# Where the low parts of a pair of hidden blocks are taken, and where w_in's sums stand, in a pooled-attention and squared-ReLU kernel

## The chip, the cores and the metric

The kernel runs on one core of one Trainium2 chip. The metric is the time of one execution in microseconds (us), the median of three runs. A profile is one more execution, recorded by the hardware profiler: its *span* goes from the first to the last instruction of the program, and its own time, as the runs are timed, includes a little around that span.

The engines of a core run side by side, each with its own queue of instructions in program order: TensorE (PE in the profile; PEld is its loading of weights), VectorE (DVE), ScalarE (ACT), GpSimd (POOL) and SyncE (SP), which issues most of the DMAs. They wait for each other through semaphores.

## The reference

Attention over keys and values that are pooled by eight, then a feed-forward block with a squared ReLU. `q`, `k`, `v` are 8 x 8 x 576 x 64 (batch, heads, sequence, width), `w_in` is 512 x 2048, `w_out` 2048 x 512, all in float32.

```python
def _attn_ref(q, k, v) -> np.ndarray:
    ...
    k_p = k.reshape(B, H, Sp, pool, D).mean(axis=3)
    v_p = v.reshape(B, H, Sp, pool, D).mean(axis=3)
    scores = scale * np.matmul(q, k_p.transpose(0, 1, 3, 2))
    scores = scores - np.max(scores, axis=-1, keepdims=True)
    attn = np.exp(scores)
    attn = attn / (np.sum(attn, axis=-1, keepdims=True) + 1e-09)
    return np.matmul(attn, v_p).astype(np.float32)

def _moe_ref(x, w_in, w_out) -> np.ndarray:
    h = np.maximum(x @ w_in, 0.0)
    return (h * h @ w_out).astype(np.float32)
```

The 4608 rows of attention output, 512 wide, are the `x` of the second function.

## The kernel before

**Chunks, blocks, steps.** The 4608 tokens are cut into nine chunks `c` of 512, the 2048 hidden columns into sixteen blocks `fc` of 128. A *step* is one chunk and one block, in the order of `steps` (line 625): step `s = 16 c + fc`. In step `s` TensorE makes block `s` of the hidden layer (`hidden`, lines 566 to 584) and then multiplies block `s - 3` with its part of `w_out` (`project`, lines 603 to 622; the 3 is `LAG`).

**Low and high parts.** From chunk 1 on each float32 operand is split in two numbers that TensorE multiplies fast: a high part (a cast on ScalarE) and a low part (the operand less its high part, on VectorE). Three products of four are made. The square of a hidden block, `r`, is so split into `gh` and `gl` by `split_hidden` (lines 586 to 594): ScalarE casts `r` into `gh` at once; the subtraction that makes `gl` is put on the list `behind`. `catch_up` (lines 176 to 178) empties that list. `r` has two buffers, `gh` and `gl` three each.

**Seven products for a pair.** Chunks 0 and 1 (`PLAIN` is 2) take each block alone (`plain`). From chunk 2 on, thus from step 32 on, `seven` (lines 526 to 564) makes two blocks at once with seven products in place of eight: an even step makes four products into two PSUM tiles X and Y and lets VectorE combine their halves (`soon`: a copy u on ScalarE, then u, h, h on VectorE; `at_end`: a second copy u, then h), the odd step makes three more. Only then are both blocks complete, and `activate` takes ReLU and square of both, r and r, on ScalarE. TensorE's next even step needs the PSUM tiles that these two free: X after the first, Y after the second.

**Operands for the seven.** `w_in` is needed in eight forms: four are its quarters (`split_quarter`, named w_A in the profile), four are sums of quarters, made in place on VectorE by `sum_of_quarters` (lines 189 to 194; wf_i) and then split by `split_operand` (lines 180 to 184; w_S). The sixteen sums are scheduled one a step, from step 27 on (line 727). The input `x` is likewise summed (xf) and split (x_B, x_T) in the last steps of the chunk before.

**Attention** for the next chunks is done between these: for each pair of heads of a chunk, `transpose_q` (qs, st) in one step, `scores` two steps later (sps, then copies sc on ScalarE, then the maximum mx over the 72 partitions on GpSimd), `exponents` two steps further (sc minus mx on VectorE, the exponential on ScalarE, then the sum tot over partitions on GpSimd), then `send_sums`, `fetch_sums`, `reciprocals`, `fetch_reciprocals` through memory (rs, rc, rr, rd, rb), and `weigh_values` (av, xf). From step 32 on scores and exponentials fall in even steps.

**What sets the order.** Every engine's order is written out: the loop over `s` (lines 763 to 810) calls the parts of a step one after the other. The places that matter here, in order: `hidden` for TensorE; fetches of weights; `split_hidden` of step `s - 2` (line 772); `project` of `s - 3`; in odd steps `catch_up` (line 778); `soon`, which in an odd step is `activate`; the ScalarE and VectorE parts of attention that follow a product; `at_end`; `catch_up` (line 785); loads; the other scheduled work; `activate` where it is not in `soon` (chunks 0 and 1); sums and operands of x, reciprocals, sums of quarters. Buffers of weights (tag "w", 40 of them) are handed out in that order as they come free, and whoever writes one waits for its last reader.

Of the kernel before, what the change touches and what calls it, by code (L numbers as in the profile page):

```python
# [37 lines left out]
def pooled_attn_relu2_ffn(  # L38
# [25 lines left out]
    NFC = DFF // P  # L64
# [8 lines left out]
    PLAIN = 2  # L73
# [31 lines left out]
    def issue_loads():  # L105
        for dst, src in loads:
            dma(dst, src)
        loads.clear()
# [6 lines left out]
    def w_tile(dt, name):  # L115
        return wts.tile([P, 2, 512], dt, name=name, tag="w", bufs=SLOTS)
# [39 lines left out]
    def to_float32(*keys):  # L156
        parts = []
        for key in keys:
            words, m = raw.pop(key).rearrange("p a (n w) -> p a n w", w=2), wf[key]
            parts.append((words, m, m.bitcast(U32)))  # L160
        for _, m, _ in parts:
            DVE.tensor_scalar(m, m, EXP_MIN, EXP_MAX, op0=ALU.max, op1=ALU.min)
        for words, _, m in parts:
            DVE.scalar_tensor_tensor(m, m, 3, words[..., 0], op0=ALU.logical_shift_left, op1=ALU.bitwise_or)
        for words, _, m in parts:
            DVE.scalar_tensor_tensor(m, words[..., 1], 0x80000000, m, op0=ALU.bitwise_and, op1=ALU.bitwise_or)

    def in_blocks(t):
        return t.rearrange("p (c r n) -> p c r n", c=2, r=GB // 2)

    def quarter(g, e, kh):
        return both(g, kh).rearrange("p c (r e n) -> p e c r n", r=GB // 2, e=2)[:, e]

    behind = []

    def catch_up():
        while behind:
            behind.pop(0)()

    def split_operand(g, name, src):  # L180
        t = wt[g, name] = w_tile(F32R, f"w_{g}_{name}")
        hi, lo = in_blocks(t[:, 0, :]), in_blocks(t[:, 1, :])
        ACT.copy(hi, src)
        behind.append(lambda: DVE.tensor_tensor(lo, src, hi.bitcast(F32), op=ALU.subtract))
# [4 lines left out]
    def sum_of_quarters(g, name):  # L189
        (e, kh), a, b, op = {"S1": ((1, 1), (1, 0), (1, 1), ALU.add), "S3": ((1, 0), (0, 0), (1, 0), ALU.subtract),  # L190
                             "S2": ((1, 1), (1, 1), (0, 0), ALU.subtract), "S4": ((0, 1), (0, 1), (1, 1), ALU.subtract)}[name]
        t = quarter(g, e, kh)
        DVE.tensor_tensor(t, quarter(g, *a), quarter(g, *b), op=op)
        behind.append(lambda: split_operand(g, name, t))

    stored = {}

# [368 lines left out]
    def hidden(c, fc):  # L566
        if c < PLAIN:
            hps = [(fc, plain(c, fc))]
        else:
            hps = seven(c, fc)  # L570
            if fc % 2 == 0:
                return hps

        def activate():
            for f, hp in hps:
                if c == 0:
                    r = gts[c, f] = sb.tile([P, CH], F32, name=f"r_{c}_{f}", tag="gl" if f % 2 else "gh", bufs=3)
                else:
                    r = gts[c, f] = sb.tile([P, CH], F32, name=f"r_{c}_{f}", tag="r", bufs=2)
                ACT.activation(r, hp, AF.Relu)  # L580
            for f, _ in hps:
                ACT.activation(gts[c, f], gts[c, f], AF.Square)

        return (activate, None, None) if c >= PLAIN else (None, None, activate)

    def split_hidden(c, fc):
        if c == 0:
            return
        gh = sb.tile([P, CH], F32R, name=f"gh_{c}_{fc}", tag="gh", bufs=3)
        gl = sb.tile([P, CH], F32R, name=f"gl_{c}_{fc}", tag="gl", bufs=3)  # L590
        r = gts[c, fc]
        gts[c, fc] = (gh, gl)
        ACT.copy(gh, r)
        behind.append(lambda: DVE.tensor_tensor(gl, r, gh.bitcast(F32), op=ALU.subtract))

    accs, outs = {}, []

    def send_outs():
        for dst, src in outs:
            dma(dst, src)  # L600
        outs.clear()

    def project(c, fc):
        if fc == 0:
            accs[c] = [ps_o.tile([P, 512], F32, name=f"o_{c}_{t}", tag=f"o{t}") for t in range(NTT)]
        g, key = gts.pop((c, fc)), ("o", fc)
        for t in range(NTT):
            tt = slice(t * P, (t + 1) * P)
            if c == 0:
                prods = [(g[:, tt], wf[key].rearrange("p a n -> p (a n)"))]  # L610
            else:
                prods = [(g[x][:, tt], wt[key][:, w, :]) for x, w in three]
            for i, (a, w) in enumerate(prods):
                PE.matmul(accs[c][t], lhsT=a, rhs=w, start=fc == 0 and i == 0, stop=fc == NFC - 1 and i == len(prods) - 1)

        def store():
            for t in range(NTT):
                ob = half_tile("ob", f"ob_{c}_{t}")
                ACT.copy(ob, accs[c][t])
                outs.append((out[c * CH + t * P:c * CH + (t + 1) * P, :], ob))  # L620

        return store if fc == NFC - 1 else None


    steps = [(c, fc) for c in range(NCH) for fc in range(NFC)]
    work = {}

    def at(step, f, *a):
        work.setdefault(max(step, -PRO), []).append((f, a))
# [22 lines left out]
    t = ps_a.tile([P, 512], F32, name="stir", tag="a")  # L652
# [60 lines left out]
    t = 1e9  # L713
    for key in reversed(keys):
        t = min(t - 1 / RATE, need[key] - 1 - MARGIN)
# [7 lines left out]
    for i in range(NFC):  # L723
        at(12 + i, split_quarter, i // GB, i % GB // 2, i % 2)
        at(10 + i, store_weights, i)
        at(11 + i, send_weights, i)
        at(27 + i, sum_of_quarters, i // 4, ("S1", "S3", "S2", "S4")[i % 4])
        for c in range(1, NCH):
            at(c * NFC + i + LAG - STREAM, fetch_weights, c, i)

# [11 lines left out]
    for c in range(1, NCH):  # L742
# [10 lines left out]
        for p in range(NPAIR):  # L753
            s = c * NFC + first[p]
# [3 lines left out]


    last = (to_float32, split_quarter, sum_of_quarters, store_weights)  # L760
    on_pe = (turn_k, scores, token_scores, token_turn, weigh_values)
    store = None
    for s in range(-PRO, len(steps) + LAG):
        todo = work.get(s, [])
        soon, then, activate = hidden(*steps[s]) if 0 <= s < len(steps) else (None, None, None)
        later = [f(*a) for f, a in sorted(((f, a) for f, a in todo if f in on_pe), key=lambda x: x[0] is weigh_values)]
        for kind in (fetch_sums, fetch_weights):
            for f, a in todo:
                if f is kind:
                    f(*a)  # L770
        if 0 <= s - 2 < len(steps):
            split_hidden(*steps[s - 2])
        if store:
            store()
            send_outs()
        store = project(*steps[s - LAG]) if s >= LAG else None
        if s % 2:
            catch_up()
        if soon:
            soon()  # L780
        for f in later:
            f()
        if then:
            then()
        catch_up()
        first = (load_q, load_sums)
        for f, a in todo:
            if f is fetch_reciprocals:
                f(*a)
        for f, a in todo:  # L790
            if f in first:
                f(*a)
        issue_loads()
        for f, a in todo:
            if f not in first + on_pe + last + (x_sums, x_operand, reciprocals, fetch_weights, fetch_sums, fetch_reciprocals, first_sums):
                f(*a)
        keys = [a[0] for f, a in todo if f is to_float32]
        if keys:
            to_float32(*keys)
        for f, a in todo:  # L800
            if f in last[1:] and f is not sum_of_quarters:
                f(*a)
        issue_loads()
        if activate:
            activate()
        for kind in (x_sums, x_operand, reciprocals, sum_of_quarters, first_sums):
            for f, a in todo:
                if f is kind:
                    f(*a)
        issue_loads()  # L810
# [32 lines left out]
```

## Time and profile before

| | before |
|---|---|
| median of three runs | 943.03 us (942.89 to 944.5) |
| the profiled execution, timed as a run | 941.49 us |
| its span | 939.7 us |
| VectorE busy | 584.8 us, 62% of the span |
| ScalarE busy | 509.1 us, 54% |
| GpSimd busy | 425.5 us, 45% |
| mean granted clock of TensorE | 0.975 |

Busy times are sums of an engine's instructions. A bracket behind a row of the timeline tells how long the engine stood idle before that row and what ended the wait. All lines of the program go through one helper, line 34, so rows are told apart by the names of their tiles: `gl<-r,gh` writes gl from r and gh. A pair of steps, one even and one odd, takes 11 to 17 us; chunk 2 begins at about 267 us of the span, chunk 3 at about 370 us.

### The profile page before, as it was taken

How to read it: one execution, taken by the hardware profiler on the slowest of the kernel's cores; microseconds unless marked ns; L12 is line 12 of the kernel's file. 1: busy time of each engine (PE TensorE's matmuls, PEld its weight loads, DVE VectorE, ACT ScalarE, POOL GpSimd, SP SyncE). 2: the span in 40 equal slices, each digit the busy share in tenths (PEclk: the TensorE clock that was granted, in tenths of full speed). 3: DMA queues.
4: the chain of work that ended last, by engine and by line, in shares of the span. 5: the costliest groups of instructions: out<-in, count | busy, mean ns of one | idle time of the engine just before them, and what ended most of it. 6: DMA issues, size and time to landing. Idle time of an engine off the chain costs nothing.

```text
span 939.7 us, 14134 instructions
## 1 busy us (share of the span) xinstructions
PE 902.5 (96%) x5050; PEld 721.0 (77%) x5050; DVE 584.8 (62%) x971; ACT 509.1 (54%) x1015; POOL 425.5 (45%) x234
## 2 busy tenths in 40 slices
PE   4799999999999999999999999999999999999998
PEld 3344444577778878888888888888888878889997
DVE  4884887466777877665867576657645764453321
ACT  2477557565556555654565556555645564344343
POOL 6662225455553666565565555566444444200000
PEclk6589999999999999999999999999999999999999
DMA  8894654688655545756565566655433343344501
GB/s 193 253 271 91 145 163 152 153 228 222 165 123 137 141 102 148 183 142 137 125 172 145 134 145 174 145 132 125 158 113 114 113 157 102 102 163 170 218 1 45
DMA packets 161623, 138.72 MB, mean 148 GB/s; under 512 B 98776, under 2 KB 126424, under 8 KB 161552
## 3 DMA queue, kind: packets, MB, share of 16 engines
q1 hardware_dynamic: 132752, 127.13, 44.6%
q0 software_dynamic: 28800, 10.68, 10.0%
q8 instruction: 40, 0.66, 0.3%
q14 instruction: 31, 0.25, 0.1%
HBM read 119.65 MB, written 18.06 MB: 147 GB/s over the span
## 4 chain that ended last, share of the span: by engine, by line
PE 73%; DVE 12%; ACT 7%; issue 4%; DMA 2%; SPq 1%; POOL 0%; DVEq 0%; ACTq 0%
PE o L34 33%; PE h L34 32%; PE av L34 3%; DVE gl L34 3%; PE sps L34 3%; ACT sc L34 2%; SPq L34 1%; DVE st L34 1%; ACT r L34 1%; DMA raw_i<-in_moe_w_in_dram 1%; DVE h L34 1%; DVE wf_i L34 1%; DVE xf L34 1%; ACT x_T L34 1%; DVE x_T L34 1%
## 5 line engine op out<-in xcount | busy, mean ns | idle before, releaser
L34 PE MATMUL o<-w_o,gh 128*128 128x512 f32 x1024 | 322.1, 396 | 0.0
L34 POOL PARTITION_ALL_REDUCE tot<-sc x56 | 187.5, 3397 | 84.9 <-issue 84.2
L34 PEld LDWEIGHTS o<-w_o,gh 128*128 128x128 f32 x1024 | 184.4, 188 | 44.0 <-issue 7.2
L34 PE MATMUL o<-w_o,gl 128*128 128x512 f32 x512 | 199.5, 390 | 0.0
L34 POOL PARTITION_ALL_REDUCE mx<-sc x56 | 115.4, 2098 | 81.4 <-ACT sc L34 76.7
L34 ACT ACTIVATE r<-h 128x512 f32<-128x512 f32 x144 | 85.5, 597 | 118.0 <-PE h L34 55.8
L34 PE MATMUL h<-x_T,w_S 128*128 128x256 f32 x1008 | 133.9, 286 | 8.2 <-ACT r L34 7.3
L34 DVE TENSOR_TENSOR gl<-r,gh 128x512 fp32r<-128x512 f32 x128 | 123.4, 977 | 27.5 <-ACT gh L34 27.3
L34 PEld LDWEIGHTS h<-x_T,w_S 128*128 128x128 f32 x1008 | 127.0, 194 | 10.2 <-ACT r L34 8.5
L34 PEld LDWEIGHTS o<-w_o,gl 128*128 128x128 f32 x512 | 96.1, 188 | 21.2
L34 DVE TENSOR_TENSOR h<-h,u 128x256 f32<-128x256 f32 x168 | 72.6, 432 | 54.5 <-ACT u L34 29.5
L34 PE MATMUL h<-x_B,w_A 128*128 128x256 f32 x672 | 98.7, 283 | 5.6 <-ACT r L34 5.6
L34 PEld LDWEIGHTS h<-x_B,w_A 128*128 128x128 f32 x672 | 91.9, 191 | 10.6 <-ACT r L34 6.4
L34 ACT COPY u<-h 128x256 f32<-128x256 f32 x112 | 41.7, 373 | 103.3 <-DVE h L34 59.0
L34 POOL DMA_DIRECT2D k<-in_k_dram x36 | 44.6, 1239 | 106.7 <-issue 47.9
L34 POOL DMA_DIRECT2D v<-in_v_dram x36 | 44.0, 1223 | 96.8 <-issue 44.8
L34 ACT ACTIVATE r<-r 128x512 f32<-128x512 f32 x144 | 84.2, 625 | 1.0
L34 DVE TENSOR_TENSOR st<-qs,st 64x512 fp32r<-64x512 f32 x56 | 44.7, 797 | 63.7 <-ACT st L34 62.9
L34 DVE TENSOR_TENSOR u<-h,u 128x256 f32<-128x256 f32 x56 | 23.2, 415 | 92.7 <-ACT u L34 92.6
L34 ACT CAST gh<-r 128x512 fp32r<-128x512 f32 x128 | 78.6, 614 | 0.8 <-PE o L34 0.4
L34 ACT ACTIVATE sc<-sc 72x512 f32<-72x512 f32 x56 | 34.5, 631 | 52.2 <-DVE sc L34 52.2
L34 PE MATMUL h<-x,wf_i 128*128 128x512 f32 x128 | 60.0, 614 | 0.1
(89 smaller groups left out, 1207.7 us busy)
## 6 DMA issues: line engine op xcount, KB each, us to landing
w_o<-kept SPq DMA_DIRECT2D x128, 512.0 KB
out_dram<-ob SPq DMA_DIRECT2D x36, 256.0 KB
raw_i<-in_moe_w_in_dram SPq DMA_DIRECT2D x16, 512.0 KB
raw_o<-in_moe_w_out_dram SPq DMA_DIRECT2D x16, 512.0 KB
kept<-w_o SPq DMA_DIRECT2D x16, 512.0 KB
rb<-rd SPq DMA_DIRECT2D x56, 128.0 KB
k<-in_k_dram POOLq DMA_DIRECT2D x36, 144.0 KB, 4.8
v<-in_v_dram POOLq DMA_DIRECT2D x36, 144.0 KB, 4.3
```

Source lines behind the costliest of these rows:

```text
L34: return lambda *a, **k: self.tc.keep_in_program_order(f(*a, **k))
```

## The change

`split_hidden` is no longer called for every block two steps after it was made. A new function, `split_at`, is called at two places of the step: at the old one with block `s - 2`, and behind `soon` with block `s - 1`. It splits an odd block of chunk 2 or later at the second place, one step after its pair was made, and every other block at the old place. So both blocks of a pair are cast in the even step behind it, and both gl are taken by the `catch_up` at the end of that even step.

The sums of w_in's quarters are scheduled from step 26 on. Their split is put on a new list, `summed`, which the loop empties behind `activate`: the cast w_S stands at the end of the step after the sum, and its low part is taken by the first `catch_up` of the step after that.

```diff
-    behind = []
+    behind, summed = [], []
...
         DVE.tensor_tensor(t, quarter(g, *a), quarter(g, *b), op=op)
-        behind.append(lambda: split_operand(g, name, t))
+        summed.append(lambda: split_operand(g, name, t))
...
         behind.append(lambda: DVE.tensor_tensor(gl, r, gh.bitcast(F32), op=ALU.subtract))
+
+    def split_at(s, f):
+        if 0 <= f < len(steps) and s - f == (1 if f % 2 and f >= PLAIN * NFC else 2):
+            split_hidden(*steps[f])
...
-        at(27 + i, sum_of_quarters, i // 4, ("S1", "S3", "S2", "S4")[i % 4])
+        at(26 + i, sum_of_quarters, i // 4, ("S1", "S3", "S2", "S4")[i % 4])
...
-        if 0 <= s - 2 < len(steps):
-            split_hidden(*steps[s - 2])
+        split_at(s, s - 2)
         if store:
             store()
             send_outs()
...
         if soon:
             soon()
+        split_at(s, s - 1)
         for f in later:
             f()
...
         if activate:
             activate()
+        while summed:
+            summed.pop(0)()
```

What this makes of the queues, at three places. In the names the last number is a buffer's; of the numbers before it the last is the block, or the operand's own index.

The first place is ScalarE at the start of chunk 3, steps 48 and 49, where chunk 2's last pair (blocks 14 and 15) is cast; - is before, + is with the change.

```order
 L34 CAST gh_14_3376<-r_14_3323 128x512
 L34 COPY u_3_0_3372<-h_0_3346 128x256
+L34 CAST gh_15_3395<-r_15_3325 128x512
 L34 COPY u_3_0_3373<-h_1_3347 128x256
-L34 ACTIVATE sc_1_3259<-sc_1_3259 72x512 x2
-L34 CAST st_2_3421<-qs_2_3419 64x512 x2
-L34 CAST gh_15_3452<-r_15_3325 128x512
+L34 ACTIVATE sc_1_3262<-sc_1_3262 72x512 x2
+L34 CAST st_2_3425<-qs_2_3423 64x512 x2
 L34 ACTIVATE r_0_3468<-h_0_3346 128x512
 L34 ACTIVATE r_1_3470<-h_1_3347 128x512
```

The cast of block 15 has moved from just ahead of the new pair's r to between the two copies u of the even step. The same place on VectorE:

```order
 L34 TENSOR_TENSOR gl_14_3377<-r_14_3323,gh_14_3376 128x512
-L34 TENSOR_TENSOR sc_1_3259<-sc_1_3259,mx_1_0_3260 72x512
-L34 TENSOR_TENSOR sc_1_3259<-sc_1_3259,mx_1_1_3261 72x512
-L34 STREAM_TRANSPOSE qs_2_3419<-q_2_3129 128x512
-L34 TENSOR_TENSOR st_2_3421<-qs_2_3419,st_2_3421 64x512 x2
-L34 TENSOR_TENSOR gl_15_3453<-r_15_3325,gh_15_3452 128x512
-L34 TENSOR_TENSOR xf_0_3444<-av_0_3445,rb_0_3398 128x512
+L34 TENSOR_TENSOR gl_15_3396<-r_15_3325,gh_15_3395 128x512
+L34 TENSOR_TENSOR sc_1_3262<-sc_1_3262,mx_1_0_3263 72x512
+L34 TENSOR_TENSOR sc_1_3262<-sc_1_3262,mx_1_1_3264 72x512
+L34 STREAM_TRANSPOSE qs_2_3423<-q_2_3133 128x512
+L34 TENSOR_TENSOR st_2_3425<-qs_2_3423,st_2_3425 64x512 x2
```

Block 15's gl stood behind sc, qs and st; it now stands directly behind block 14's and ahead of them.

The second place is ScalarE in steps 32 and 33, the first pair of chunk 2. Before:

```order
L34 COPY u_2_0_2252<-h_1_2226 128x256
L34 CAST w_S_2276<-wf_i_1_506 128x512
L34 ACTIVATE sc_1_2137<-sc_1_2137 72x512 x2
L34 CAST st_2_2303<-qs_2_2301 64x512 x2
L34 CAST gh_15_2335<-r_15_2205 128x512
L34 CAST w_S_2350<-wf_i_0_479 128x512
L34 ACTIVATE r_0_2354<-h_0_2225 128x512
L34 ACTIVATE r_1_2356<-h_1_2226 128x512
```

With the change:

```order
L34 COPY u_2_0_2255<-h_1_2229 128x256
L34 ACTIVATE sc_1_2140<-sc_1_2140 72x512 x2
L34 CAST st_2_2304<-qs_2_2302 64x512 x2
L34 CAST w_S_2309<-wf_i_0_479 128x512
L34 CAST gh_15_2338<-r_15_2206 128x512
L34 ACTIVATE r_0_2355<-h_0_2228 128x512
L34 ACTIVATE r_1_2357<-h_1_2229 128x512
```

The cast w_S from wf_i_0_479 stands ahead of gh, and its sum was made one step earlier. VectorE there, before:

```order
L34 TENSOR_TENSOR st_2_2303<-qs_2_2301,st_2_2303 64x512 x2
L34 TENSOR_TENSOR wf_i_0_479<-wf_i_0_479 128x4x128
L34 TENSOR_TENSOR gl_15_2336<-r_15_2205,gh_15_2335 128x512
L34 TENSOR_TENSOR w_S_2350<-wf_i_0_479,w_S_2350 128x512
L34 TENSOR_TENSOR xf_0_2327<-av_0_2328,rb_0_2280 128x512
```

With the change:

```order
L34 TENSOR_TENSOR st_2_2304<-qs_2_2302,st_2_2304 64x512 x2
L34 TENSOR_TENSOR wf_i_1_506<-wf_i_1_506,wf_i_0_479 128x4x128
L34 TENSOR_TENSOR w_S_2309<-wf_i_0_479,w_S_2309 128x512
L34 TENSOR_TENSOR gl_15_2339<-r_15_2206,gh_15_2338 128x512
L34 TENSOR_TENSOR xf_0_2330<-av_0_2331,rb_0_2281 128x512
```

The sum in this place is now that of the next operand, and gl_15, a block of chunk 1, has changed places with the low part of w_S.

The third place is ScalarE in steps 42 and 43, where the last w_S is cast. Before:

```order
L34 COPY u_2_10_2963<-h_11_2937 128x256
L34 CAST w_S_3004<-wf_i_1_968 128x512
L34 CAST gh_9_3035<-r_9_2930 128x512
L34 CAST w_S_3050<-wf_i_1_968 128x512
L34 ACTIVATE r_10_3054<-h_10_2936 128x512
L34 ACTIVATE r_11_3056<-h_11_2937 128x512
```

With the change:

```order
L34 COPY u_2_10_2966<-h_11_2940 128x256
L34 CAST w_S_3017<-wf_i_1_968 128x512
L34 ACTIVATE r_10_3054<-h_10_2939 128x512
L34 ACTIVATE r_11_3056<-h_11_2940 128x512
```

The last cast w_S, block 9's gh and the w_S before it have all left the stretch between the even step's second copy and r; what stands there is the last w_S alone, in the even step. Its buffer is another one too: before, it came from the weights of block 8, which step 43's `project` reads, now from those of block 7, read in step 42.

## The prediction

> **What bounds the kernel now.** I read the page first, then TensorE's own waits, then the waits of all engines, then the timeline around each stall. TensorE is busy for 96% of the span and carries 73% of the chain, so the change can only win what TensorE stands idle for, plus time at a lowered clock.
>
> ```profile
> PE 902.5 (96%) x5050; PEld 721.0 (77%) x5050; DVE 584.8 (62%) x971; ACT 509.1 (54%) x1015; POOL 425.5 (45%) x234
> ...
> PE 73%; DVE 12%; ACT 7%; issue 4%; DMA 2%; SPq 1%; POOL 0%; DVEq 0%; ACTq 0%
> ```
>
> The waits of TensorE alone (who, for whom, us in total, times, longest) are short after the start of the kernel:
>
> ```profile
> PE h L34 <- ACT r L34: 12.9, 8, 4.4
> ...
> PE h L34 <- DVE x_T L34: 0.6, 2, 0.3
> PE h L34 <- ACT x_T L34: 0.3, 1, 0.3
> ```
>
> Eight waits of 12.9 us for the activation r, and three of 0.9 us for x_T, are what this change can reach. What holds r up is, on ScalarE, gl:
>
> ```profile
> ACT r L34 <- DVE gl L34: 51.4, 26, 3.4
> L34 DVE TENSOR_TENSOR gl<-r,gh x128: 674/682/3677, 179.5 to 928.2; 128x512 fp32r<-128x512 f32 x128
> ```
>
> A gl takes 682 ns by the median and up to 3677 ns. One of the six steady cases, in the timeline (start, us, engine, operation, idle before it):
>
> ```profile
> 471.23 0.68 DVE L34 TENSOR_TENSOR gl<-r,gh 128x512 fp32r<-128x512 f32 x1
> ...
> 473.34 6.59 POOL L34 PARTITION_ALL_REDUCE tot<-sc  x2 [0.97 <-issue]
> ...
> 474.42 2.42 DVE L34 TENSOR_TENSOR st<-qs,st 64x512 fp32r<-64x512 f32 x2 [0.69 <-ACT st L34]
> 475.58 0.59 ACT L34 ACTIVATE r<-h 128x512 f32<-128x512 f32 x1
> 476.87 2.62 DVE L34 TENSOR_TENSOR gl<-r,gh 128x512 fp32r<-128x512 f32 x1
> 477.17 0.88 PE L34 MATMUL h<-x_B,w_A 128*128 128x256 f32 x6
> 479.41 0.68 DVE L34 TENSOR_TENSOR xf<-av,rb 128x512 f32<-128x512 f32 x1
> 479.58 0.60 ACT L34 ACTIVATE r<-h 128x512 f32<-128x512 f32 x1 [3.41 <-DVE gl L34]
> 480.23 1.69 PE L34 MATMUL h<-x_T,w_S 128*128 128x256 f32 x12 [1.47 <-ACT r L34]
> ```
>
> GpSimd's sum over partitions (tot) starts at 473.3; the VectorE operations that run beside it, st and then gl, take 2.42 for two and 2.62 for one. The second r has to wait for gl, because r has two buffers and gl reads the older one. TensorE's next pair may write its second PSUM tile only after that r, and stands for 1.47 us.
>
> **Part 1: the odd block's gh and gl one step earlier.** Nothing is added or removed, and no transfer moves: of 128 gh and 128 gl, the 56 of odd blocks in chunks 2 to 8 stand earlier. In the odd steps from step 35 on, r then finds both gl done in the step before. In the case above gl would end at about 472.5, the cast gh leaves ScalarE's odd step, the exponentials and casts of st start 0.6 later, so the first r stays near 475.6 and the second ends at 476.8 instead of 480.2. TensorE needs it 1.42 us (two groups of six, 0.71 each from 477.17 to the next row) after 477.17, at 478.6: the stall goes, with 1.8 to spare. The six steady stalls together are 12.9 less the two below, 4.36 and 1.20: **7.3 us**, all taken as won.
>
> The three waits for x_T, at two starts of a chunk, hang on the same chain:
>
> ```profile
> 463.26 0.60 ACT L34 ACTIVATE r<-h 128x512 f32<-128x512 f32 x1 [1.58 <-DVE gl L34]
> ...
> 464.79 0.61 ACT L34 CAST x_T<-xf 128x512 fp32r<-128x512 f32 x1
> 465.45 0.38 PE L34 MATMUL h<-x_T,w_S 128*128 128x256 f32 x1 [0.28 <-ACT x_T L34]
> ```
>
> r waited 1.58 for gl, and the cast of x_T stands behind r; it comes some 0.9 earlier. **0.9 us**.
>
> What the move puts in the way: in the even step one cast of 0.6 ahead of the copies of the scores, and one gl of 0.68 ahead of sc minus mx, so tot, SyncE's queue behind it and the next weights come 0.7 later.
>
> ```profile
> 407.81 3.32 SPq L34 DMA_DIRECT2D rs<-tot  x2
> ...
> 409.57 1.07 ACT L34 COPY sc<-sps 72x512 f32<-72x512 f32 x2 [1.59 <-PE sps L34]
> ...
> 413.67 0.38 SPq L34 DMA_DIRECT2D w_o<-kept  x1
> ...
> 420.50 0.30 PEld L34 LDWEIGHTS o<-w_o,gh 128*128 128x128 f32 x2
> w_o<-kept SPq DMA_DIRECT2D x128, 512.0 KB
> ```
>
> The cast falls in the 1.59 that ScalarE waits for TensorE there. SyncE waits for tot (3.32 in one issue) with the next w_o behind it; that w_o is issued at 413.67 and first used at 420.50. At the 158 GB/s of a window's row further down, its 512 KB would take 3.3 us, an estimate, which leaves 3.5: a delay of 0.7 costs nothing. So **0**; without that cover it would be up to 0.7 in each of the 24 score steps from step 32 on.
>
> **Part 2: w_in's sums at step 26, casts behind r.** Sixteen sums, casts and splits only move. Two stalls are in their range. In step 43 the cast of w_S stands ahead of r on ScalarE and waits for a buffer that TensorE still reads:
>
> ```profile
> 345.24 0.62 ACT L34 CAST w_S<-wf_i 128x512 fp32r<-128x512 f32 x1 [5.06 <-PE o L34]
> ...
> 346.40 0.98 PE L34 MATMUL h<-x_B,w_A 128*128 128x256 f32 x6 [1.20 <-ACT r L34]
> ```
>
> Now that last cast stands at the end of step 42 and its buffer comes free with that step's product, around 340, before step 43's blocks are summed: **1.2 us** won.
>
> The largest stall is step 34's:
>
> ```profile
> 279.42 0.39 PE L34 MATMUL o<-w_o,gl 128*128 128x512 f32 x1
> ...
> 280.32 2.64 DVE L34 TENSOR_TENSOR wf_i<-wf_i 128x512 f32<-128x512 f32 x1
> 282.88 0.68 DVE L34 TENSOR_TENSOR gl<-r,gh 128x512 fp32r<-128x512 f32 x1
> 282.99 0.62 ACT L34 CAST w_S<-wf_i 128x512 fp32r<-128x512 f32 x1 [3.85 <-DVE wf_i L34]
> 283.52 1.08 ACT L34 ACTIVATE r<-h 128x512 f32<-128x512 f32 x2
> 284.16 0.97 PE L34 MATMUL h<-x_B,w_A 128*128 128x256 f32 x6 [4.36 <-ACT r L34]
> 284.97 3.81 PE L34 MATMUL h<-x_T,w_S 128*128 128x256 f32 x18
> ...
> 297.92 2.32 PE L34 MATMUL h<-x_T,w_S 128*128 128x256 f32 x18
> ```
>
> Here the cast no longer waits: the first r follows the casts of st, w_S and gh (before, the cast of w_S was free to start 3.85 before 282.99, at 279.1; with gh behind it that makes r 279.7 to 280.3), and TensorE starts its first tile there. But block 31 belongs to the plain chunks, so its gl is **not** moved: it still stands in step 33 behind wf_i, and now behind the split of w_S too, as long as a gl. It ends at about 284.3, the second r at 284.9. TensorE runs 12 products from 280.3 and goes on at 284.9; before it was at that point at 284.97 plus a third of 3.81, 286.2. That gives 1.3. What follows depends on the clock. The rows by window (stretch, length, busy us and instructions of PE, PEld, DVE, ACT and POOL, then granted clock, DMA share, GB/s) show full clock, then half:
>
> ```profile
> 281.90:285.00 3.10, 0.84 (x7) 0.84 (x8) 3.02 (x5) 2.01 (x4) 1.51 (x1) 1.00 0.30 120
> 285.00:288.40 3.40, 3.40 (x19) 3.40 (x18) 0.96 (x2) 1.51 (x4) 0.00 (x0) 0.50 0.46 158
> ```
>
> Halved, the 18 took 3.81 where 2.32 is usual. The new idle time is 0.5 and then 3.2, nearer to 4.36 (clock halved) than to the 1.47 at 480.23 (behind it 12 products took 1.69, the full rate), so I take it halved again: the 12 left take 2.5, h ends near 287.4 and not 288.8, less some 0.4 for the score products that now run slow too: **1.0 us**. Bounds: 0, if VectorE is held longer, and 5.9, all of the idle time and the 1.5 of the clock.
>
> [...]
>
> **Sum.** 7.3 + 0.9 + 1.2 + 1.0 = 10.4 us. The profiled execution took 941.49 (span 939.7 and 1.8 around it), so it would take 931.1; the median of the three runs, 943.03, lies 1.5 above it. I forecast the median: 943.0 - 10.4 = **932.6**.
>
> **The rivals.** *Clock stays full in step 34.* The 12 products and the scores run at their usual rate: 2.3 instead of 1.0, so 931.3. For it: the stall of 1.47 did not halve the clock. Against it: the two windows above.
>
> *The blocking finds a new victim.* GpSimd's sums still run; what VectorE executes then is slow. In the case above that would be st, xf or the sums in the odd step. If the score products wait for xf, or the next pair for u, up to 1.0 at each chunk start comes back, five times: 937.6. Against it is the row of h in the view of one tile (least, median and longest ns):
>
> ```profile
> L34 DVE TENSOR_TENSOR h<-h,u x168: 431/433/433, 272.4 to 921.4; 128x256 f32<-128x256 f32 x168
> ```
>
> None of 168 was ever slowed, nor was the xf at 479.41, beside tot; both read PSUM and one SBUF tile, while the slow gl, st and wf_i read two.
>
> *The moved pair is caught by the maxima: slower.* In a score step the two gl now stand at the end, beside mx. If one is blocked by each of the two, the second ends with mx:
>
> ```profile
> 743.59 3.96 POOL L34 PARTITION_ALL_REDUCE mx<-sc  x2 [2.71 <-ACT sc L34]
> ...
> 750.77 0.88 PE L34 MATMUL h<-x_B,w_A 128*128 128x256 f32 x6
> ```
>
> mx ends at 747.6; the second r, 0.6 long, must end by 750.8 + 1.42, so gl by 751.6. It decides only if gl comes 4 us later than that. Each us beyond costs 24 us over the score steps; 0.6 beyond (14 us) makes 946.9, slower than before.
>
> [...]
>
> *It does not do what it says:* r waits for something else just behind gl. ScalarE's row before it, r at 475.58, was done at 476.2, and h's products, the other thing that r needs, end before 475.58 too, so I see nothing; then 942.
>
> **How the numbers follow.** Forecast 0.56 (932.6), full clock 0.22 (931.3), new victim 0.12 (937.6), no effect 0.05 (942), slower 0.05 (946.9). Run to run the medians may move by the 1.5 seen. The range goes from 931.3 less 1.5 and a little of step 34's upper bound, 929.0, to the new victim, 937.6. A measurement of this kernel can tell about 0.2% (1.9 us) from no change: faster 0.90, same 0.05, slower 0.05.
>
> **What would show it.** In the profile after: no row "ACT r <- DVE gl" beyond a few us, where 51.4 stood; TensorE's waits for r down to one or two, at step 34, near 3 us; none at the chunk starts; no PE wait for w_S or behind it in step 43; gl still up to 3 us long in places, but in even steps. Wrong would be: new TensorE waits for xf, u, gl or w_o of over 2 us in sum, a longer r chain in even steps, or a step 34 that still stands 4 us.

## The result, and the profile after

| | before | with the change |
|---|---|---|
| median (lowest to highest) | 942.86 us (937.59 to 944.5, 6 runs) | 935.01 us (933.7 to 938.82, 6 runs) |
| ratio | | 0.993, 95% interval 0.9901 to 0.996 |
| profiled execution, its span | 941.49, 939.7 | 938.82, 937.0 |
| VectorE busy | 584.8 us | 571.3 us |

The kernel became 7.9 us faster; 10.4 had been forecast (932.6, range 929.0 to 937.6).

The profiled executions of the changed kernel and of the run called *three r, sums* below are the longest of their six runs, and the latter had a granted clock of 0.95 from 470.8 to 484.8 us, where the kernel before, three r and no tot show 1.00 at the same place, and a mean of 0.928, where all others have 0.971 to 0.996. The changed kernel's reached step 32 at 273.26 us, the one of before at 267.53, with nearly the same work ahead; so the two are compared from step 32 on. The profile after, first the shares of the chain, then TensorE's waits (engine, tile and line, waited for: us in total, times, longest), then ScalarE's wait for gl:

```profile
PE 80%; DVE 7%; DMA 4%; ACT 3%; issue 3%; SPq 1%; POOL 0%; DVEq 0%; ACTq 0%
...
PE h L34 <- ACT r L34: 3.4, 2, 3.0
...
PE o L34 <- DMA w_o<-kept: 1.4, 2, 1.0
PE h L34 <- DVE x_T L34: 0.7, 2, 0.3
...
PE h L34 <- DVE h L34: 0.2, 1, 0.2
PE h L34 <- ACT x_T L34: 0.2, 1, 0.2
...
ACT r L34 <- DVE gl L34: 11.3, 4, 4.1
```

TensorE's eight waits for r (12.9 us) have become two, both in step 34; in their place stands a wait for the weights w_o that was not there. ScalarE's wait for gl fell from 51.4 to 11.3. The place that the prediction showed in the old trace, step 65, now reads so (timeline: start, us, engine, operation, idle before it):

```profile
474.75 1.28 DVE L34 TENSOR_TENSOR gl<-r,gh 128x512 fp32r<-128x512 f32 x2
...
477.46 6.59 POOL L34 PARTITION_ALL_REDUCE tot<-sc  x2 [0.17 <-issue]
...
478.54 2.42 DVE L34 TENSOR_TENSOR st<-qs,st 64x512 fp32r<-64x512 f32 x2 [0.68 <-ACT st L34]
...
479.17 1.09 ACT L34 ACTIVATE r<-h 128x512 f32<-128x512 f32 x2
...
481.66 2.32 PE L34 MATMUL h<-x_T,w_S 128*128 128x256 f32 x18
```

Both gl are taken at 0.64 each before tot begins; beside tot VectorE now does st, 2.42 for the two, and then xf (0.69) and u (0.42), which take their usual time (0.69 and 0.42 by the median). The two r follow one another, and the 18 products run without a break where 1.47 us of idle time stood.

The starts of pairs of steps (a pair's first product h<-x_B,w_A on TensorE) cut every trace into stages. The nine experiments of the next section are in the table too. The medians of the kernel before in their comparisons were 942.13 (gl alone, sums alone, three r, block 31 too), 941.42 (three r and sums, w_o first, no tot) and 943.41 (the two with q cut). In us:

| kernel | steps 32 to 35 | steps 42, 43 | steps 32 to 47 | step 48 to the end | median |
|---|---|---|---|---|---|
| before | 29.68 | 13.86 | 102.20 | 569.97 | 942.86 |
| the change | 30.16 | 11.71 | 101.05 | 562.69 | 935.01 |
| gl alone | 29.68 | 12.92 | 101.28 | 564.14 | 934.98 |
| sums alone | 31.04 | 12.60 | 102.20 | 572.61 | 942.13 |
| three r | 29.69 | 13.20 | 101.54 | 561.15 | 934.03 |
| block 31 too | 26.36 | 11.77 | 97.17 | 564.97 | 932.30 |
| three r, sums | 25.27 | 11.91 | 95.81 | 563.69 | 929.52 |
| block 31, w_o first | 26.35 | 11.49 | 97.24 | 567.97 | 935.24 |
| no tot | 25.24 | 12.83 | 96.93 | 562.33 | 925.98 |
| q cut in two | 31.18 | 11.52 | 102.14 | 561.74 | 933.58 |
| three r, sums, q cut | 25.31 | 11.94 | 95.83 | 561.38 | 926.61 |

From step 48 on the change won 7.28; in steps 32 to 47 only 1.15. There the first two pairs, with step 34, became 0.48 longer. TensorE after the change, at the start of step 33 and in step 34, with the VectorE and ScalarE rows it waits for:

```profile
280.35 0.95 PE L34 MATMUL h<-x_B,w_S 128*128 128x256 f32 x6 [0.24 <-DVE h L34]
...
284.78 2.41 DVE L34 TENSOR_TENSOR st<-qs,st 64x512 fp32r<-64x512 f32 x2 [0.69 <-ACT st L34]
...
287.10 0.98 PE L34 MATMUL h<-x_B,w_A 128*128 128x256 f32 x6 [0.41 <-ACT r L34]
287.20 2.64 DVE L34 TENSOR_TENSOR wf_i<-wf_i,wf_i 128x512 f32<-128x512 f32 x1
...
290.37 0.68 DVE L34 TENSOR_TENSOR gl<-r,gh 128x512 fp32r<-128x512 f32 x1
...
291.14 0.60 ACT L34 ACTIVATE r<-h 128x512 f32<-128x512 f32 x1 [4.09 <-DVE gl L34]
...
291.79 2.79 PE L34 MATMUL h<-x_T,w_S 128*128 128x256 f32 x12 [2.99 <-ACT r L34]
```

It is the stall that the prediction described (first r free, second r behind block 31's gl, which stands behind a slow wf_i), but it ends later than the prediction said. And the new wait for w_o, at the start of chunk 3: SyncE's queue (DMA issues) and TensorE:

```profile
380.96 5.02 SPq L34 DMA_DIRECT2D q<-in_q_dram  x8
386.07 1.01 SPq L34 DMA_DIRECT2D w_o<-kept  x2
...
391.37 0.73 PE L34 MATMUL o<-w_o,gh 128*128 128x512 f32 x2 [1.05 <-DMA w_o<-kept]
```

The first of the two w_o is issued behind eight loads of q, and TensorE has to wait for it 5.3 us later.

### The profile page after: what moved, and what is told of

It reads as the page before. It is cut to its first block, busy times and chain, and to the rows that moved or that the text cites. A ratio compares the mean times of both kernels' runs of the same rounds, so it can differ in the third digit from the quotient of the medians.

```text
span 937.0 us, 14129 instructions
## 1 busy us (share of the span) xinstructions
PE 904.6 (97%) x5050; PEld 722.5 (77%) x5050; DVE 571.3 (61%) x971; ACT 508.5 (54%) x1015; POOL 420.1 (45%) x234
## 4 chain that ended last, share of the span: by engine, by line
PE 80%; DVE 7%; DMA 4%; ACT 3%; issue 3%; SPq 1%; POOL 0%; DVEq 0%; ACTq 0%
PE o L34 38%; PE h L34 35%; PE av L34 4%; PE sps L34 3%; SPq L34 1%; DVE wf_i L34 1%; DVE gl L34 1%; DMA w_o<-kept 1%; ACT sc L34 1%; DMA raw_i<-in_moe_w_in_dram 1%; DVE tm L34 1%; DVE kl L34 1%; DMA rb<-rd 1%; DVE st L34 0%; DMA v<-in_v_dram 0%
## 5 line engine op out<-in xcount | busy, mean ns | idle before, releaser
L34 POOL PARTITION_ALL_REDUCE mx<-sc x56 | 110.6, 2018 | 62.8 <-ACT sc L34 60.3
L34 ACT ACTIVATE r<-h 128x512 f32<-128x512 f32 x144 | 83.3, 594 | 96.5 <-PE h L34 76.0
L34 DVE TENSOR_TENSOR gl<-r,gh 128x512 fp32r<-128x512 f32 x128 | 91.7, 752 | 5.8 <-ACT gh L34 5.7
L34 DVE TENSOR_TENSOR st<-qs,st 64x512 fp32r<-64x512 f32 x56 | 48.6, 868 | 61.1 <-ACT st L34 60.3
L34 PE MATMUL o<-wf_o,r 128*128 128x512 f32 x128 | 60.4, 616 | 0.0
```

The source lines that it names most:

```text
L34: return lambda *a, **k: self.tc.keep_in_program_order(f(*a, **k))
```

## The experiments

Each ran with the kernel before on the same chip; ratios are to that, with their 95% interval.

**The two halves of the change.** *gl alone* keeps `split_at` at both places and puts the sums back:

```diff
-        summed.append(lambda: split_operand(g, name, t))
+        behind.append(lambda: split_operand(g, name, t))
...
-        at(26 + i, sum_of_quarters, i // 4, ("S1", "S3", "S2", "S4")[i % 4])
+        at(27 + i, sum_of_quarters, i // 4, ("S1", "S3", "S2", "S4")[i % 4])
```

> Only the odd block's gh and gl stand one step earlier; w_in's sums and their casts stand where they stood before. Theory A (the odd gl, blocked beside GpSimd's tot, held r, and that alone made the steady stalls): from step 48 to the end 7.3 us less than before, as in the changed kernel; in chunk 2 the stall of step 43/44 (1.2) and that of step 34 (4.4) stay, so the median is 6 to 8 us under the kernel before, ratio 0.992 to 0.994. Rival B (the sums' new place carries a good part, by what it clears in chunk 2): under 4 us, ratio above 0.996.

Measured: 934.98, ratio 0.9921 (0.9894 to 0.9948). Its TensorE waits:

```profile
PE h L34 <- ACT r L34: 5.6, 2, 4.4
...
PE o L34 <- DMA w_o<-kept: 2.3, 3, 1.2
```

The two waits for r are step 34's 4.35 and step 44's 1.20, as before; the six steady ones are gone. Moving gl alone gives what the whole change gives. From step 48 on it wins 5.83, less than the 7.3 expected, with 2.3 us of new waits for w_o, all three at starts of chunks. *Sums alone* has the change's sums and `split_hidden` at `s - 2` throughout:

```diff
-        if 0 <= f < len(steps) and s - f == (1 if f % 2 and f >= PLAIN * NFC else 2):
+        if 0 <= f < len(steps) and s - f == 2:
```

> Only w_in's sums start at step 26 with their casts at the end of a step; both gl stand where they stood before. Theory A: the stall of step 43/44 goes (1.2), step 34 keeps a stall of about 4 us because block 31's gl still stands behind a slow wf_i, and the six steady stalls and the 51 us of r waiting for gl stay: 0 to 2 us under the kernel before, ratio 0.998 to 1.000. Rival B: 4 us or more, ratio under 0.996.

Measured: 942.13, ratio 1.0002 (0.9982 to 1.0021): nothing. The pair of steps 42 and 43 became 1.26 shorter, as expected, but steps 32 to 35 became 1.36 longer. (From step 48 on it took 2.64 longer, with 2.39 us of waits for x_T where 0.90 stood; what moved them is not shown.) The products and the granted clock (PEclk) there; the first two rows are of the timeline, the others of the view by windows (stretch, length, busy us and instructions of PE, PEld, DVE, ACT, POOL, then PEclk, DMA share, GB/s):

```profile
280.58 0.87 PE L34 MATMUL h<-x_T,w_S 128*128 128x256 f32 x6
284.46 2.93 PE L34 MATMUL h<-x_T,w_S 128*128 128x256 f32 x12 [3.01 <-ACT r L34]
...
283.00:284.00 1.00, 0.00 (x0) 0.00 (x0) 1.00 (x3) 0.19 (x1) 0.00 (x0) 0.78 0.01 2
284.00:290.00 6.00, 5.54 (x23) 5.26 (x24) 2.21 (x5) 4.19 (x10) 1.00 (x1) 0.50 0.29 92
290.00:291.00 1.00, 1.00 (x5) 0.77 (x5) 0.99 (x3) 1.00 (x3) 1.00 (x2) 0.81 0.00 0
```

A stall of 3.0 us in place of 4.36 was followed by twice as long a stretch at half clock: 6.8 us (0.44 + 6 + 0.38, the edges from 0.78 and 0.81), against 3.4 in the kernel before.

**Is it the buffer, or the place?** *Three r* is the kernel before with one more buffer of r, one less of gh (for chunk 0's even blocks too, which use the same buffers) and no instruction moved:

```diff
-                    r = gts[c, f] = sb.tile([P, CH], F32, name=f"r_{c}_{f}", tag="r", bufs=2)
+                    r = gts[c, f] = sb.tile([P, CH], F32, name=f"r_{c}_{f}", tag="r", bufs=3)
...
-        gh = sb.tile([P, CH], F32R, name=f"gh_{c}_{fc}", tag="gh", bufs=3)
+        gh = sb.tile([P, CH], F32R, name=f"gh_{c}_{fc}", tag="gh", bufs=2)
```

> The kernel before with r in three buffers in place of two (and gh in two in place of three, to make room); every instruction stands where it stood. Theory A (r waits for gl only because gl still reads the buffer that r wants): ScalarE's wait of r for gl falls from 51 us to a few, the six steady stalls and the waits for x_T go though gl is as slow as before and as late, and the median is 6 to 8 us under the kernel before; step 34 keeps its stall, since there the cast of w_S waits for wf_i ahead of r. Rival C (the stall comes from the place of the cast and of gl in the odd step, not from the buffer): under 2 us, with TensorE's waits for r still above 10 us; a buffer of gh less may cost waits of ScalarE for TensorE.

Measured: 934.03, ratio 0.9912 (0.9885 to 0.9938). The row of gl in the view of one tile (least, median and longest ns), TensorE's waits for r, and ScalarE's wait with one gh less:

```profile
L34 DVE TENSOR_TENSOR gl<-r,gh x128: 676/683/3698, 178.8 to 920.9; 128x512 fp32r<-128x512 f32 x128
...
PE h L34 <- ACT r L34: 5.6, 2, 4.4
...
ACT gh L34 <- PE o L34: 80.1, 57, 2.5
```

gl is as slow as it was (3698 ns at the longest, 3677 before) and stands where it stood, yet the steady stalls are gone, and ScalarE has no wait of r for gl left in its list. So a slow gl harmed only through the buffer that it still read. With one buffer of gh less ScalarE waits 80.1 us for TensorE (57 times, 2.5 at most), without a stall of TensorE behind it. *No tot*, again on the kernel before, takes the other link away; it leaves out the sum over partitions and divides by one row of the exponentials:

```diff
-            GP.partition_all_reduce(tots[i], sc[:, i], channels=SP_, reduce_op=bass_isa.ReduceOp.add)
...
-            dma(rs[i:i + 1], tots[i][0:1])
+            dma(rs[i:i + 1], sc[0:1, i])
```

> The kernel before without GpSimd's sum over partitions tot: the reciprocals are taken from one row of the exponentials. All else, the two buffers of r and the late odd gl too, stands as before. Theory A (gl is late only because it runs beside tot): gl takes 0.68 us at most wherever it stood beside tot, the six steady stalls of TensorE go, and the median is 6 to 9 us under the kernel before. Rival C (the odd gl is late by its place, behind st and the cast gh): TensorE's waits for r stay above 8 us, under 3 us won.

Measured: 925.98, ratio 0.9831 (0.9809 to 0.9853), more than expected, because step 34 shrinks as well: its r waited behind a wf_i that took 2.64 us beside tot (280.32 to 282.96, tot until 283.40) and takes 0.69 without. The rows of gl and st:

```profile
L34 DVE TENSOR_TENSOR gl<-r,gh x128: 676/683/930, 180.0 to 915.6; 128x512 fp32r<-128x512 f32 x128
L34 DVE TENSOR_TENSOR st<-qs,st x56: 684/687/690, 116.0 to 763.5; 64x512 fp32r<-64x512 f32 x56
```

Without tot no gl takes over 0.93 us and no st over 0.69. The chain tot, slow VectorE operation, late release of r, stalled TensorE is shown at both ends.

**Step 34.** *Block 31 too* is the changed kernel with the last plain block split early as well:

```diff
-        if 0 <= f < len(steps) and s - f == (1 if f % 2 and f >= PLAIN * NFC else 2):
+        if 0 <= f < len(steps) and s - f == (1 if f % 2 and f >= PLAIN * NFC - 1 else 2):
```

> The changed kernel, with block 31 (the last plain block) split one step earlier too. Theory A (step 34 still stands 3.0 us because block 31's gl was not moved, and its idle time halves the clock behind it): TensorE's wait for r at step 34 falls from 3.0 to under 0.7 and the clock in the 3.5 us behind it stays full: 3 to 4.5 us under the changed kernel. Rival D (the blocking finds a new victim: with gl of block 31 gone ahead, wf_i or the x operands of steps 32 and 33 come late in its place): under 1 us, and a new wait for u, h, x_T or w_S in steps 32 to 35. Between them (clock halved for some other idle time): 1 to 3 us.

Measured: 932.30, ratio 0.9906 (0.9873 to 0.9938). ScalarE and the clock at step 34 (timeline, then windows as above):

```profile
279.55 0.62 ACT L34 CAST w_S<-wf_i 128x512 fp32r<-128x512 f32 x1
280.07 1.08 ACT L34 ACTIVATE r<-h 128x512 f32<-128x512 f32 x2
...
280.00:284.00 4.00, 4.00 (x32) 3.82 (x31) 3.96 (x4) 2.19 (x5) 4.00 (x2) 1.00 0.87 270
```

No wait for r is left, the clock stays full, and steps 32 to 35 take 3.80 less than with the change, as theory A said. In step 34 the score products now wait 0.85 for xf, which stands on VectorE behind the slow wf_i (2.64 us): that much of rival D came. Only part of the 3.80 reached the end, 2.7 by the medians: from step 48 on this kernel took 2.28 longer, where TensorE waits three times for w_o (0.24, 0.70 and 0.79 us) and three times for x_T (0.17, 0.34 and 0.34).

**The waits for w_o.** *Block 31, w_o first* adds to that kernel, in steps with loads of q from step 32 on, the next step's fetch of w_o ahead of them:

```diff
+        if s >= 32 and any(f is load_q for f, a in todo):
+            for f, a in work.get(s + 1, []):
+                if f is fetch_weights:
+                    f(*a)
+            work[s + 1] = [x for x in work.get(s + 1, []) if x[0] is not fetch_weights]
         for f, a in todo:
             if f in first:
```

> The changed kernel with block 31 split early too, and from step 32 on the next step's w_o is fetched ahead of a step's eight loads of q, not behind them. Theory W (the moved pair pushes SyncE's queue back, and a w_o that stands behind the eight q loads comes late now that no stall for r covers it): TensorE's waits for w_o fall from 2.7 to under 0.5 us: 929 to 931. Rival E (the fetch now waits for a buffer ahead of the q loads, so q, then st and the scores come late): 932 or more, with waits for q or sps. Rival F (w_o is late for want of transfer rate, wherever it is issued): the waits stay above 2 us.

Measured: 935.24, ratio 0.994 (0.9914 to 0.9965); theory W fell in this form. SyncE at the start of chunk 3, then TensorE's waits for w_o:

```profile
373.48 0.58 SPq L34 DMA_DIRECT2D w_o<-kept  x1
374.10 6.72 SPq L34 DMA_DIRECT2D q<-in_q_dram  x8
380.97 0.34 SPq L34 DMA_DIRECT2D w_o<-kept  x1
385.47 3.48 SPq L34 DMA_DIRECT2D rs<-tot  x2
389.88 0.34 SPq L34 DMA_DIRECT2D rc<-rs  x1
390.32 0.38 SPq L34 DMA_DIRECT2D w_o<-kept  x1
...
PE o L34 <- DMA w_o<-kept: 3.2, 4, 1.0
```

The fetch that had been late now is in time, but the eight q loads behind it take 6.72 us to issue, and TensorE, earlier at the next pair, waits 0.81 us at 394.15 for the w_o that is issued at 390.32, behind SyncE's wait for tot. The waits moved on. In sum they are 3.2 us, as rival F expected; whether the transfer rate has a part in them this run does not show. *q cut in two* is the changed kernel with the eight loads spread over two steps:

```diff
-            at(s - 2 if c < PLAIN else max(s - QL, 6), load_q, c, p)
+            if c <= PLAIN:
+                at(s - 2 if c < PLAIN else max(s - QL, 6), load_q, c, p)
+            else:
+                at(s - QL, load_q, c, p, (0,))
+                at(s - QL + 1, load_q, c, p, (1,))
```

> The changed kernel with each chunk's eight q loads of a head pair cut in two: four in the step where they stood, four in the step behind it, so that the next w_o stands behind four of them, not eight. Theory W2 (w_o is late at the start of chunk 3 because SyncE reaches it only after some 5 us of q loads): that w_o is issued about 2 us earlier after the start of the pair, and TensorE's waits for w_o fall from 1.4 to under 0.5 us; 1 to 1.5 us under the changed kernel. Theory F2 (the bytes of that stretch, 2.4 MB in 14 us, decide, and the order in SyncE's queue does not; what was hidden by the old stall for r now shows): the waits stay near 1 to 1.5 us or move to the w_o after it, and the time stays within 1 us of the changed kernel.

Measured: 933.58, ratio 0.9877 (0.9846 to 0.9908). The same stretch:

```profile
376.44 2.06 SPq L34 DMA_DIRECT2D q<-in_q_dram  x4
378.54 1.18 SPq L34 DMA_DIRECT2D w_o<-kept  x1
379.76 2.40 SPq L34 DMA_DIRECT2D q<-in_q_dram  x4
382.26 0.49 SPq L34 DMA_DIRECT2D w_o<-kept  x1
...
PE o L34 <- DMA w_o<-kept: 0.6, 1, 0.6
```

The pair starts at 369.76 here and at 374.31 with the change; that w_o is issued 8.8 us after the start in place of 11.8, and the wait of 1.05 is gone (the 0.6 left is another, in step 44). That speaks for W2; 1.4 us between medians of different sets of runs do not show it by time.

**Together.** *Three r, sums* is the three-r kernel with the sums of the change; *three r, sums, q cut* adds the cut loads. Both are made of edits shown above.

> r in three buffers (gh in two), and w_in's sums from step 26 with their casts at the end of a step; gh and gl of odd blocks stand where they stood before the change. Theory A: the steady stalls are gone with the third buffer; in step 34 neither the cast of w_S (moved) nor block 31's gl (its buffer is not wanted) stands ahead of r, so the first two pairs of chunk 2 take about 26.4 us as with block 31 split early, not 29.7; the stall of step 43/44 goes; and w_o is in time, since the scores' side is not pushed back: about 5 us under the kernel with three r alone, 927.5 to 931. Rival D (the sums' place costs elsewhere: alone it made the first two pairs 1.4 longer and the waits for x_T 2 us more): 932 or more, with new waits for x_T, u or h in steps 32 to 50.

> Three buffers of r and w_in's sums from step 26, as in the run of that name, with the q loads cut in two as well. Theory W2: its one wait for w_o of 0.8 us goes, 928 to 929.5. Theory F2: no change, 929 to 930.5. Either way about 5 to 6 us under the changed kernel, since step 34, step 43/44 and the steady stalls are all clear.

Measured: 929.52, ratio 0.9875 (0.9844 to 0.9906), and 926.61, ratio 0.9811 (0.978 to 0.9842). With a third r block 31's gl no longer matters and the sums' new place pays: steps 32 to 35 take 25.3, not 29.7. In the trace at the lower clock, the first of the two still waits 0.8 for w_o at the start of chunk 3 although no gl was moved; the second has no wait for w_o. Of the second one's waits these lie in step 32 or later (of the first row only the longer one):

```profile
PE sps L34 <- DVE xf L34: 1.6, 2, 1.0
PE h L34 <- ACT r L34: 0.4, 1, 0.4
...
PE h L34 <- DVE x_T L34: 0.3, 1, 0.3
```

The last kernel, faster than its expectation, is 8.4 us under the change by the medians, and the two intervals do not meet.

## Why the prediction was right or wrong

- **Six steady stalls, 7.3 us: right, and for the reason given.** All six are gone, with gl moved, with a third r and without tot alike. From step 48 on the three-r kernel, which has no wait for w_o, wins 8.82 (569.97 less 561.15), somewhat more than the waits of before there (five stalls of 6.53 and three for x_T of 0.90): a stall costs its wait and 0.15 to 0.3 around it (the pair of steps 66 and 67, 13.19 with one of 1.47, takes 11.58 without).
- **x_T at chunk starts, 0.9: wrong, the sum of these waits stayed.** It was 0.90 and is 0.89. The pairs at 464 and 561 us of the old trace held 0.28 + 0.34 and 0.28 of waiting. The first is clear now. The second keeps 0.34, though no r waits for gl anywhere near it, and 0.15 of it stays with three r too: that wait did not hang on gl. Chunk 2's start has new ones of 0.21 and 0.34. There the sums' cast stands ahead of that of x_T, behind an r that waits 2.31 for gl; the kernel with gl alone has none at that place, nor have the two with three r and the sums, so it takes both.
- **Step 43/44, 1.2: right.** With the sums alone that pair takes 1.26 less, with gl alone 0.94 less, with both 2.15.
- **Step 34, +1.0: wrong, it cost 0.5.** The steps "first r at 280.3" and "clock halved again" held. What failed is "It ends at about 284.3, the second r at 284.9": that is 17.4 us after the start of the stage at 267.53, and it came 18.5 after it (291.74 less 273.26). Step 33's products began 7.09 after the start of the stage, not 5.94; 0.55 of that are the new waits for x_T, which the sums alone make too (6.82 there, while the kernel with gl alone keeps 5.94), and 0.24 is a wait for h that no other run has there. The chain on VectorE, two slow st (2.41 us together), a slow wf_i (2.64), the split of w_S, then gl, came that much later. So the 1.3 us that the shorter stall should have given became 0.1 (TensorE went on 18.5 after the start of the stage; before it was at that point after 18.7), the score products behind it ran at half clock as predicted (the granted clock was 0.50 from 292 to 295 us), and the balance was a loss. How large a loss was luck: with the sums alone and with q cut, which stall there for the same 3.0 us, steps 32 to 35 lost 1.36 and 1.50, by a second stretch at half clock.
- **The later tot, SyncE's queue and w_o, 0: wrong, it cost 1.05 of waits.** The working took one place, where 3.5 us lay between landing and use, for all places, and its estimate of 3.3 for the landing is too short for others: at the start of chunk 3 the product that waits begins 5.30 after its w_o is issued. At the start of a chunk w_o stands behind eight q loads, with almost nothing to spare. In the kernel before it was issued 11.53 after the pair's start, and TensorE came to that product 5.32 later, at 16.85, held up by a stall for r of 1.07; after the change it is issued at 11.76, TensorE comes at 16.0 and waits to 17.06. The delay that I priced is only a part of it: w_o also comes late, by 0.6 and 0.8, in the run without tot, where no gl was moved. The stall that the change removes was a part of the cover, not all of it: the three-r kernel has no stall there either, issues that w_o at 10.86 and uses it at 15.53 without a wait. Cutting the q loads takes that wait away.
- **A wait that no term had: w_o in step 44, 0.37.** VectorE, SyncE, GpSimd and TensorE after the change:

```profile
344.12 4.09 POOL L34 PARTITION_ALL_REDUCE mx<-sc  x2
346.49 2.13 DVE L34 TENSOR_TENSOR gl<-r,gh 128x512 fp32r<-128x512 f32 x2
348.54 0.68 DVE L34 TENSOR_TENSOR w_S<-wf_i,w_S 128x512 fp32r<-128x512 f32 x1
349.25 0.34 SPq L34 DMA_DIRECT2D w_o<-kept  x1
353.86 0.73 PE L34 MATMUL o<-w_o,gh 128*128 128x512 f32 x2 [0.37 <-DMA w_o<-kept]
```

  The moved pair of gl runs beside the maxima and takes 2.13 in place of 1.28; the split of the last w_S stands behind it, and SyncE waits 3.4 us for that split before it issues the next w_o (in the kernel before it waited 0.9 there, for TensorE). Neither gl alone nor the sums alone makes TensorE wait there; with q cut, which has both, it waits 0.62.
- **The rivals.** The clock did not stay full (0.50 behind step 34's stall). The blocking did find other operations: st above all (up to 3.90 us for two, at 572.72), in places wf_i (2.64 at 287.20), w_S (2.75 at 312.46) and sums of x (up to 2.85 us for one xf); outside step 34 TensorE waits for none of them. The maxima did catch the moved gl, at eight places, but only for 0.3 to 1.0 us each, and TensorE waited behind one of them, in step 44.
- **The sum.** In steps 32 to 47, 3.0 had been forecast (1.0 + 1.2 + 0.76 for the one steady stall there) and 1.15 came: 1.5 missing in steps 32 to 35, 0.37 in step 44. From step 48 on 7.4 had been forecast and 7.28 came, but not from the forecast terms alone: 0.34 of the waits for x_T stayed, 1.05 went to w_o, and by luck the gain above the sum of the waits paid for both.

## What to carry to other kernels

A late reader of a shared buffer can be moved or given one more buffer; here the buffer was worth as much (0.9912 and 0.993, with intervals that overlap), and it left every queue's order as it was. Before a delay is called hidden, look for its narrowest place, not a typical one, and ask whether a part of the cover is the very stall that the change removes. Two parts of a change can work against each other or only together: the sums alone won nothing and beside the moved gl nothing that can be measured, with a third r about 4.5 us by the medians, though these two intervals overlap.

## What the runs showed of the hardware

Behind step 34's stall the granted clock was at half for 3.4 us in the kernel before and in the changed one, and for 6.8, twice that, with the sums alone, whose stall was shorter than that of before (3.0 against 4.36). The length of the stall does not decide which: with q cut step 34 stalls for 0.41 and 3.00 us, as in the changed kernel (0.41 and 2.99), and the clock there was at half for at least 6.0 us (5.04 of the first row, all of the second; the columns are as above):

```profile
284.00:290.00 6.00, 3.92 (x19) 3.86 (x20) 3.83 (x8) 3.49 (x8) 0.58 (x1) 0.58 0.34 104
290.00:291.00 1.00, 1.00 (x6) 0.87 (x5) 0.00 (x0) 0.78 (x2) 0.37 (x1) 0.50 0.00 0
```

TensorE was not idle all through the 3.4 us ahead of a fall: with the sums alone those ahead of the fall at 283.56 hold 1.3 us of products (280.15 to 281.45). The next 3.4 us hold 2.5 us of products, and the clock stayed at half for as long again. What makes it fall, and for how long, these runs do not show.

Eight loads of q take SyncE 5.02 us to issue after the change, 4.2 to 5.8 at that place in the other kernels that issue them in a row, and 6.72 where a fetch of 512 KB was issued just ahead of them.

Beside tot single VectorE operations with two SBUF inputs, gl, st and wf_i among them, took up to 3.7 us in place of 0.68; without tot no gl took over 0.93. None of the 168 h, which have one input in PSUM, took over 0.433, before or after. By the recorded starts the slow operation can be the earlier one: in the kernel before, a gl that began at 379.78, ahead of tot at 380.17, took 3.59, and the gl of 2.62 in step 65 began at 476.87, behind tot at 473.34.
